# Chunked attention with two feed-forwards: an attention pair in thirteen short steps, GpSimd's lower parts in four pieces, and every second tile of the first feed-forward on ScalarE

## The chip, the cores and the metric

One core of a Trainium2 chip runs the whole program. The metric is device time in microseconds (us) of one execution, shown as the median of several runs. The engines are called as in the profile: PE is TensorE, DVE is VectorE, ACT is ScalarE, POOL is GpSimd, and SP is the engine whose queue issues most transfers. Each engine takes its own instructions strictly in order and waits for the others by semaphores.

## What is computed

Attention within chunks of 64 tokens, then two feed-forwards of 4608 tokens, width 512 and inner width 2048, in float32:

```python
def _attn_ref(q, k, v):            # q, k, v: (8, 8, 576, 64), chunks of 64
    scores = scale * np.matmul(q_c, k_c.transpose(0, 1, 2, 4, 3))
    scores = scores - np.max(scores, axis=-1, keepdims=True)
    attn = np.exp(scores)
    attn = attn / (np.sum(attn, axis=-1, keepdims=True) + 1e-09)
    out = np.matmul(attn, v_c)

def _moe_ref(x, w_in, w_out, s, b):
    r = np.maximum(x @ w_in, 0.0)
    return (s * (r * r) + b) @ w_out

def _moe2_ref(x, w_in, w_out):
    h = x @ w_in
    return (h * (1.0 / (1.0 + np.exp(-1.702 * h)))) @ w_out
```

## The kernel before, in words

The tokens are cut into nine blocks of 512. A product in full precision is made of three matmuls in a reduced type: each operand is split into an upper part (`hi`, `gh`, `xh`) and a lower part (`lo`, `gl`, `xl`), and lo x hi, hi x hi and hi x lo are summed in PSUM.

A block of a feed-forward runs over 16 slices i of the inner width. `gemm_in` makes h for one slice with twelve matmuls of 128x512 (line 519), two PSUM banks in turn. In the first feed-forward, h becomes g = s * relu(h)^2 + b and is split (lines 531 to 536): ACT makes r = relu(h), DVE r = s * r * r, ACT the upper part gh = r + b, and DVE the lower part gl = (r + b) - gh. `gemm_out` takes gh and gl, again with twelve matmuls (line 594), two slices later (`LAG`), so that on PE the slices' products alternate: twelve for h of slice i + 2, twelve for the output of slice i. There are three buffers for gh and gl.

While the first feed-forward of blocks 2 to 8 runs, three other works share the engines. The attention of the blocks still to come is done in pairs of heads (class `Pair`, a generator whose steps are placed in time by `plan_attention`, four pairs to a block): q and k are transposed in blocks of 32x32 by DVE (line 272, `qt` and `kt`), PE makes the scores (line 307), DVE subtracts the maxima and later divides by the sums (lines 316 to 329), ACT makes the exponential (line 322), DVE transposes the result with eight instructions (`turn`, line 281, `pt`), PE makes the products with v (line 292), and ACT and DVE split them (`split_x`). Second, the weights of the second feed-forward come as 64-bit numbers in two halves: SP loads them into a staging buffer `wst` (lines 112 and 118), ACT and DVE decode them into `wm` (lines 124 to 134), POOL adds (line 136) and writes them to DRAM (line 182). Third, `sums` reads four quarters of two such weights back (line 195), POOL makes sums of them (lines 198 to 201), copies the seven results to upper parts (line 203), makes the lower parts (line 204), and writes both to DRAM (line 209). `wst` has three buffers, which loads and sums take in turn. One round of this work takes two weights (the first and the second decoding) and two sums, and there are 16 rounds, 13.3 units of the plan apart (32 units are a block, two are a slice).

Then come the second feed-forward of block 0 and, from some 1050 us on, that of the other eight blocks in pairs, by products of sums of quarters (class `Halves`), which reads what `sums` wrote.

What sets the order: the plan gives every item a place in time, the code is written out in that order, and the language's scheduler then orders the instructions of each engine by its own estimate of when each could run. The steps of a pair that are due at one time are written together. `tmp` has ten buffers for all passing tiles of 128x512.

Names: `r`, `gh`, `gl` as above; `p` the scores, `sm` their sums, `pt` the transposed scores; `wst` and `wm` the staged and the decoded weight; `acc` the PSUM banks of the outputs; `ost` the output on its way to DRAM.

Of the kernel before, what the change touches and what calls it, by code (L numbers as in the profile page):

```python
# [8 lines left out]
F32 = mybir.dt.float32  # L9
F32R = mybir.dt.float32r  # L10
# [14 lines left out]


FIRST_STEPS = (0, 0.6, 0.8, 1.1, 1.8, 2.4, 2.7, 3.6, 3.9, 4.5)
LAG = 2
STAGED = 8
OPS = 4  # L30
# [16 lines left out]
def chunk_attention_two_ffn(ctx, tc, q, k, v, w1_in, w1_out, s, b, w2_in, w2_out, out):  # L47
# [50 lines left out]
    def split(hi, lo, src):  # L98

        nc.scalar.activation(out=hi, in_=src, func=AF.Copy)  # L100
        nc.vector.tensor_tensor(out=lo, in0=src, in1=hi.bitcast(F32), op=ALU.subtract)


    def tmp(name, dtype=F32):
        return tpool.tile([P, NB_MAX], dtype, tag="tmp", name=name)
# [83 lines left out]
    def sums(kind, i, z):  # L189

        q = staged().rearrange("p f z -> p (f z)").bitcast(F32).rearrange("p (t c) -> p t c", c=P)
        one, two = ((1, 2), (0, 3)) if kind == "wi" else ((1, 0), (2, 3))
        for t, (a, b) in ((i, one), (i + KF // 2, two)):
            for c, to in ((z, a), (2 + z, b)):
                nc.sync.dma_start(out=q[:, to, :], in_=w2_dram[kind][t][:, c * P:(c + 1) * P])
        yield
        a21, a11, a12, a22, s1, s2, s3, s4 = (q[:, t, :] for t in range(8))
        nc.gpsimd.tensor_tensor(out=s1, in0=a21, in1=a22, op=ALU.add)
        nc.gpsimd.tensor_tensor(out=s3, in0=a11, in1=a21, op=ALU.subtract)
        nc.gpsimd.tensor_tensor(out=s2, in0=s1, in1=a11, op=ALU.subtract)  # L200
        nc.gpsimd.tensor_tensor(out=s4, in0=a12, in1=s2, op=ALU.subtract)
        hi = staged().rearrange("p f z -> p (f z)").bitcast(F32R).rearrange("p (t c) -> p t c", c=P)[:, 0:7, :]
        nc.gpsimd.tensor_copy(out=hi, in_=q[:, 1:8, :])
        nc.gpsimd.tensor_tensor(
            out=q[:, 1:8, :].bitcast(F32R), in0=q[:, 1:8, :], in1=hi.bitcast(F32), op=ALU.subtract
        )
        to = wi_sums[i][:, :, z] if kind == "wi" else wo_sums[:, :, i, z]
        for part, src in enumerate((hi.bitcast(F32), q[:, 1:8, :])):
            nc.gpsimd.dma_start(out=to[:, :, part, :], in_=src)
# [26 lines left out]
    class Pair:  # L236
# [32 lines left out]
        def stage_qk(self):  # L269
            self.qt, self.kt = tmp("qt")[:, 0:self.n], tmp("kt")[:, 0:self.n]  # L270
            for t, src in ((self.qt, self.raw[0]), (self.kt, self.raw[1])):
                nc.vector.transpose(out=t.rearrange("p (u l) -> p u l", l=BK), in_=src)
            yield
            yield

        def turn(self, p):
            pt = tmp("pt")[:, 0:self.n].rearrange("p (c t) -> p c t", t=CH)
            for r in heads:
                for eq in range(2):
                    for ek in range(2):  # L280
                        nc.vector.transpose(  # L281
                            out=pt[r.start + ek * BK:r.start + (ek + 1) * BK, :, eq * BK:(eq + 1) * BK],
                            in_=p[r.start + eq * BK:r.start + (eq + 1) * BK, :, ek * BK:(ek + 1) * BK],
                        )
            return pt

        def room_scores(self):
            return left
# [12 lines left out]
        def steps(self):  # L301

            yield from self.stage_qk()
            yield
            ps = self.room_scores().rearrange("p e (c t) -> p e c t", t=CH)
            for e, i, c, h, r, other in quarters(self.nch):
                nc.tensor.matmul(  # L307
                    out=ps[other, e, i, :], lhsT=self.qt[r, c * CH:(c + 1) * CH], rhs=self.kt[r, c * CH:(c + 1) * CH],
                    start=True, stop=True,
                )  # L310
            yield
            mx = spool.tile([P, self.nch], F32, tag="mx", name="mx")
            sm = spool.tile([P, self.nch], F32, tag="sm", name="sm")
            p = tmp("p")[:, 0:self.n].rearrange("p (c t) -> p c t", t=CH)
            by_bank = mx.rearrange("p (e c) -> p e c", e=2)
            nc.vector.tensor_reduce(out=by_bank, in_=ps, axis=AX.X, op=ALU.max)
            nc.vector.tensor_tensor(
                out=p.rearrange("p (e c) t -> p e c t", e=2), in0=ps,
                in1=by_bank.unsqueeze(3).to_broadcast([P, 2, self.nch // 2, CH]), op=ALU.subtract,
            )  # L320
            yield
            nc.scalar.activation(out=p, in_=p, func=AF.Exp, scale=scale)
            yield
            nc.vector.tensor_reduce(out=sm, in_=p, axis=AX.X, op=ALU.add)
            nc.vector.tensor_scalar(out=sm, in0=sm, scalar1=1e-9, scalar2=None, op0=ALU.add)
            nc.vector.reciprocal(out=sm, in_=sm)
            nc.vector.tensor_tensor(  # L327
                out=p, in0=p, in1=sm.unsqueeze(2).to_broadcast([P, self.nch, CH]), op=ALU.mult
            )
            yield  # L330
            turned = self.turn(p)
            yield
            self.second(turned)
            yield
            self.split_x()
            done[0, self.j] = done.get((0, self.j), 0) + 1

    class EarlyPair(Pair):
# [21 lines left out]
        def turn(self, p):  # L360
            ps = acc_ps.tile([P, self.n], F32, tag=f"acc{2 * (self.hp % 2)}", name="pT")
            for i in range(self.n // P):
                nc.tensor.transpose(
                    ps[:, i * P:(i + 1) * P], p[:, 2 * i:2 * i + 2, :].rearrange("p c t -> p (c t)"), ident
                )
            pt = tmp("pt")[:, 0:self.n]
            nc.vector.tensor_copy(out=pt, in_=ps)
            return pt.rearrange("p (c h q) -> p c h q", h=2, q=CH)


        def room_scores(self):
# [95 lines left out]
    def steps_at(times, make, after_x=False):  # L467

        st = {}

        def step(n):
            g = st.setdefault("g", make())
            traced = nc.cur_bb.bb.instructions
            old = len(traced)
            for _ in range(n):
                next(g, None)
            for ins in traced[old:] if after_x else ():
                if ins.engine in first_x:
                    tc.add_manual_dep(ins, first_x[ins.engine].name, IN_ORDER, reason="behind the first x")
        for t, n in times:  # L480
            at(t, step, n)

    def plan_attention(j):

        base = NS * (j - 1)
        for p in range(HP):
            pr, o = Pair(j, p), base + (-6 + 8 * p if j == 2 else 7 * p - 3)
            at(o - 6.5, pr.load_qk)
            at(o + 2.5, pr.load_v)
            steps_at(((o - 2, 3), (o + 1, 1), (o + 2, 4), (o + 8, 1), (o + 8.5, 1)), pr.steps)  # L490

    def plan_y(j):
        base = NS * (NBLK + j - 1)
# [17 lines left out]
    def gemm_in(f, j, i):  # L511
        n = sizes[j]
        hi, lo = W[f, "wi", i]
        assert done[f, j] == KD
        ps = h_ps.tile([P, n], F32, tag="h", name="h")
        for kk in range(KD):
            xh, xl = X[f, j, kk]
            for a, (w_, x_) in enumerate(((lo, xh), (hi, xh), (hi, xl))):
                nc.tensor.matmul(  # L519
                    out=ps, lhsT=w_[:, kk, :], rhs=x_,  # L520
                    start=kk == 0 and a == 0, stop=kk == KD - 1 and a == 2,
                )
        if f == 0 and j < 2:
            if (j, i) == (0, 1):
                first_x[mybir.EngineType.PE] = nc.cur_bb.bb.instructions[-1]
            return keep_square(j, i, ps)
        gh = gpool.tile([P, n], F32R, tag="gh", name="gh")
        gl = gpool.tile([P, n], F32R, tag="gl", name="gl")
        r = tmp("r")[:, 0:n]
        if f == 0:  # L530
            nc.scalar.activation(out=r, in_=ps, func=AF.Relu)  # L531
            nc.vector.scalar_tensor_tensor(out=r, in0=r, scalar=s_ap, in1=r, op0=ALU.mult, op1=ALU.mult)  # L532
            nc.scalar.activation(out=gh, in_=r, func=AF.Identity, bias=b_ap)  # L533
            nc.vector.scalar_tensor_tensor(  # L534
                out=gl, in0=r, scalar=b_ap, in1=gh.bitcast(F32), op0=ALU.add, op1=ALU.subtract
            )
        else:
            nc.scalar.activation(out=r, in_=ps, func=AF.Sigmoid, scale=1.702)
            nc.vector.tensor_tensor(out=r, in0=ps, in1=r, op=ALU.mult)
            split(gh, gl, r)  # L540
        return gh, gl
# [411 lines left out]
```

## Time and profile before

| | us |
|---|---|
| median of 3 runs | 1676.16 (1675.64 to 1676.69) |
| the profiled execution's own time | 1671.44 |
| its span, first to last instruction | 1669.6 |

| engine | busy us | share of the span |
|---|---|---|
| PE | 1592.9 | 95% |
| PE's weight loads | 1293.2 | 77% |
| DVE | 1183.2 | 71% |
| ACT | 720.6 | 43% |
| POOL | 364.9 | 22% |

The shares are means over stages that differ. A busy PE also counts matmuls at the lower of its two clock levels (1.2 GHz instead of 2.4), so the granted clock is read beside it; a clock of 0.98 means that a small part of the stretch ran at half speed. In a timeline, the number in brackets is the idle time of the engine in front of the instruction, with what ended it.

### The profile page before, as it was taken

To read this page: it belongs to the slowest core of one execution; us is meant where nothing else is said; L and a number is where in the kernel's file an instruction comes from. 1 tells how busy PE (TensorE), PEld (TensorE's weight loads), DVE (VectorE), ACT (ScalarE), POOL (GpSimd) and SP (SyncE) were. 2 spreads that over 40 slices of the span, in tenths; PEclk is the share of its full clock that TensorE was granted. 3 is DMA by queue.
4 is the path that set the end of the run, shared out by engine and by line. 5 is a ranking of instruction groups with operands and counts; after the bars stand their busy time and mean duration, and the time that the engine had idled before them with its cause. 6 is when DMAs were issued, how large, how long until landed. Compare 5 with 4: busy or idle time off the path is not lost.

```text
span 1669.6 us, 24650 instructions
## 1 busy us (share of the span) xinstructions
PE 1592.9 (95%) x8928; PEld 1293.2 (77%) x8928; DVE 1183.2 (71%) x1832; ACT 720.6 (43%) x1222; POOL 364.9 (22%) x390
## 2 busy tenths in 40 slices
PE   5889999999999999899999999999999999999998
PEld 4668877787877788678888888888887888788876
DVE  5786757878766787777866644469667956894685
ACT  3668634323322333223334533446345534553552
POOL 1322101444444434344454210000000000100000
PEclk8889999999999999899999999999999999999999
DMA  9425444545455454545337551576767686768663
GB/s 231 110 101 149 129 130 124 149 136 152 124 145 137 120 151 126 149 127 151 103 118 223 167 161 35 182 227 228 201 210 251 195 224 204 243 180 239 209 202 76
DMA packets 348937, 272.19 MB, mean 163 GB/s; under 512 B 256144, under 2 KB 288912, under 8 KB 348816
## 3 DMA queue, kind: packets, MB, share of 16 engines
q1 hardware_dynamic: 333200, 220.28, 47.3%
q0 software_dynamic: 13312, 46.15, 8.3%
q10 hardware_dynamic: 2304, 4.20, 0.7%
q8 instruction: 70, 1.15, 0.3%
q14 instruction: 51, 0.42, 0.1%
HBM read 209.72 MB, written 60.82 MB: 162 GB/s over the span
## 4 chain that ended last, share of the span: by engine, by line
PE 51%; DVE 1%; ACT 0%; issue 0%; ACTq 0%
PE x L789 10%; PE x L694 10%; PE acc L594 7%; PE h L519 7%; PE at L694 5%; PE at L789 5%; PE b L694 3%; PE b L789 3%; DVE wo L716 0%; DVE pt L281 0%; ACT r L715 0%; PE at L292 0%; PE at L307 0%; DVE p L327 0%; DVE gl L534 0%
## 5 line engine op out<-in xcount | busy, mean ns | idle before, releaser
L519 PE MATMUL h<-xh,wi 128*128 128x512 f32 x1280 | 404.5, 398 | 10.0 <-ACT r L549 8.6
L594 PE MATMUL acc<-gh,wo 128*128 128x512 f32 x1152 | 363.0, 403 | 15.3 <-ACT gh L533 8.8
L519 PEld LDWEIGHTS h<-xh,wi 128*128 128x128 f32 x1280 | 242.3, 191 | 63.8 <-ACT r L549 10.1
L594 PEld LDWEIGHTS acc<-gh,wo 128*128 128x128 f32 x1152 | 220.8, 194 | 65.1 <-ACT gh L533 10.6
L519 PE MATMUL h<-xl,wi 128*128 128x512 f32 x640 | 251.9, 394 | 0.0
L594 PE MATMUL acc<-gl,wo 128*128 128x512 f32 x576 | 225.4, 402 | 12.3 <-DVE gl L534 12.2
L533 ACT ACTIVATE gh<-r,sb 128x512 fp32r<-128x512 f32 x112 | 80.9, 723 | 235.0 <-DVE r L532 234.7
L534 DVE SCALAR_TENSOR_TENSOR gl<-r,sb,gh 128x512 fp32r<-128x512 f32 x112 | 113.2, 1012 | 50.7 <-ACT gh L533 50.7
L594 PEld LDWEIGHTS acc<-gl,wo 128*128 128x128 f32 x576 | 111.3, 193 | 40.6 <-DVE gl L534 17.1
L519 PEld LDWEIGHTS h<-xl,wi 128*128 128x128 f32 x640 | 122.1, 191 | 26.2
L630 POOL DMA_DIRECT2D xr<-y x32 | 17.6, 549 | 506.7 <-ACT r L715 242.4
L532 DVE SCALAR_TENSOR_TENSOR r<-r,sb 128x512 f32<-128x512 f32 x112 | 109.0, 976 | 21.8 <-ACT r L531 21.3
L136 POOL TENSOR_TENSOR wm<-wm,wc 128x512 int32<-128x512 int32 x52 | 77.8, 1498 | 211.1 <-DVE wm L134 140.4
L716 DVE TENSOR_TENSOR wo<-wo,r 128x512 f32<-128x512 f32 x96 | 66.1, 692 | 74.4 <-ACT r L715 74.0
L766 ACT ACTIVATE op<-wo 128x512 fp32r<-128x512 f32 x128 | 80.1, 631 | 79.3 <-PE x L789 28.2
L789 PE MATMUL x<-op,wi 128*128 128x512 f32 x432 | 105.1, 389 | 0.0
L281 DVE STREAM_TRANSPOSE pt<-p 32x256 f32<-32x256 f32 x224 | 97.7, 436 | 4.1
L531 ACT ACTIVATE r<-h 128x512 f32<-128x512 f32 x112 | 65.8, 587 | 77.7 <-PE h L519 69.4
L694 PE MATMUL x<-xh,wi 128*128 128x512 f32 x320 | 99.0, 389 | 0.0
L715 ACT ACTIVATE r<-wo 128x512 f32<-128x512 f32 x96 | 60.8, 633 | 88.2 <-DVE wo L713 87.4
L767 DVE TENSOR_TENSOR op<-wo,op 128x512 fp32r<-128x512 f32 x128 | 86.0, 680 | 11.8 <-ACT op L766 10.4
L789 PEld LDWEIGHTS x<-op,wi 128*128 128x128 f32 x432 | 81.1, 188 | 16.8
(149 smaller groups left out, 2786.5 us busy)
## 6 DMA issues: line engine op xcount, KB each, us to landing
wi<-wo_sums SPq DMA_DIRECT2D x112, 512.0 KB, 3.8
wi<-wi_sums SPq DMA_DIRECT2D x96, 512.0 KB, 3.6
wst<-in_moe_w_out SPq DMA_DIRECT2D x32, 512.0 KB, 3.8
wi_sums<-wst POOLq DMA_DIRECT2D x32, 448.0 KB, 4.3
wo_sums<-wst POOLq DMA_DIRECT2D x32, 448.0 KB, 4.2
wst<-in_moe_w_in SPq DMA_DIRECT2D x24, 512.0 KB, 4.2
y<-ost SPq DMA_DIRECT2D x36, 256.0 KB, 3.2
xr<-y POOLq DMA_DIRECT2D x32, 256.0 KB, 4.4
```

The lines of the kernel that those rows point to most:

```text
L136: nc.gpsimd.tensor_tensor(out=t, in0=t, in1=c.bitcast(I32), op=ALU.add)
L281: nc.vector.transpose(out=pt[r.start + ek * BK:r.start + (ek + 1) * BK, :, eq * BK:(eq + 1) * BK], in_=p[r.start + eq * BK:r.start + (eq + ...
L519: nc.tensor.matmul(out=ps, lhsT=w_[:, kk, :], rhs=x_, start=kk == 0 and a == 0, stop=kk == KD - 1 and a == 2,)
L532: nc.vector.scalar_tensor_tensor(out=r, in0=r, scalar=s_ap, in1=r, op0=ALU.mult, op1=ALU.mult)
L533: nc.scalar.activation(out=gh, in_=r, func=AF.Identity, bias=b_ap)
L534: nc.vector.scalar_tensor_tensor(out=gl, in0=r, scalar=b_ap, in1=gh.bitcast(F32), op0=ALU.add, op1=ALU.subtract)
L594: nc.tensor.matmul(out=acc[m], lhsT=l_, rhs=r_, start=i == 0 and a == 0, stop=i == KF - 1 and a == 2)
L694: nc.tensor.matmul(out=self.ps[key], lhsT=l_, rhs=r_, start=start and k == 0 and a == 0, stop=k == HK - 1 and a == 2, skip_group_check=not ...
L716: nc.vector.tensor_tensor(out=g, in0=h, in1=r, op=ALU.mult)
L766: nc.scalar.activation(out=hi, in_=src, func=AF.Copy)
L767: nc.vector.tensor_tensor(out=lo, in0=src, in1=hi.bitcast(F32), op=ALU.subtract)
L789: nc.tensor.matmul(out=self.ps[key], lhsT=l_, rhs=r_, start=start and i == 0 and a == 0, stop=i == HF - 1 and a == 2, skip_group_check=not ...
```

## The change

Three edits, on DVE, POOL and ACT. A pair's steps are given one by one with times of their own (`PAIR_STEPS`, in plan units from the pair's place), where they were given in five groups: the two transposes of q and k at -2 and -1.5, the scores at 1, maximum and subtraction at 1.9, the exponential at 2.2, the division at 3, the eight transposes in twos at 3.7, 4.2, 4.7 and 5.2, the second product at 8 and the split at 8.5 (maximum to last transpose were all at 2). The early pairs of blocks 0 and 1 have the same number of steps as before, at the same times. POOL's lower parts of 7 x 128 columns are made with four instructions, of two, two, two and one tile of 128 columns. In the first feed-forward of blocks 2 to 8, the odd slices (56 of 112) get r = r^2 and then s * r + b on ACT, and `split`: the upper part by an ACT copy and the lower by a DVE subtraction.

```diff
@@ -25,6 +25,7 @@
 
 
 FIRST_STEPS = (0, 0.6, 0.8, 1.1, 1.8, 2.4, 2.7, 3.6, 3.9, 4.5)
+PAIR_STEPS = (-2, -1.5, -1, 1, 1.9, 2.2, 3, 3.7, 4.2, 4.7, 5.2, 8, 8.5)
 LAG = 2
 STAGED = 8
 OPS = 4
@@ -201,9 +202,12 @@
         nc.gpsimd.tensor_tensor(out=s4, in0=a12, in1=s2, op=ALU.subtract)
         hi = staged().rearrange("p f z -> p (f z)").bitcast(F32R).rearrange("p (t c) -> p t c", c=P)[:, 0:7, :]
         nc.gpsimd.tensor_copy(out=hi, in_=q[:, 1:8, :])
-        nc.gpsimd.tensor_tensor(
-            out=q[:, 1:8, :].bitcast(F32R), in0=q[:, 1:8, :], in1=hi.bitcast(F32), op=ALU.subtract
-        )
+
+        for t0, t1 in ((0, 2), (2, 4), (4, 6), (6, 7)):
+            nc.gpsimd.tensor_tensor(
+                out=q[:, 1 + t0:1 + t1, :].bitcast(F32R), in0=q[:, 1 + t0:1 + t1, :], in1=hi[:, t0:t1, :].bitcast(F32),
+                op=ALU.subtract,
+            )
         to = wi_sums[i][:, :, z] if kind == "wi" else wo_sums[:, :, i, z]
         for part, src in enumerate((hi.bitcast(F32), q[:, 1:8, :])):
             nc.gpsimd.dma_start(out=to[:, :, part, :], in_=src)
@@ -270,11 +274,11 @@
             self.qt, self.kt = tmp("qt")[:, 0:self.n], tmp("kt")[:, 0:self.n]
             for t, src in ((self.qt, self.raw[0]), (self.kt, self.raw[1])):
                 nc.vector.transpose(out=t.rearrange("p (u l) -> p u l", l=BK), in_=src)
-            yield
-            yield
+                yield
 
         def turn(self, p):
-            pt = tmp("pt")[:, 0:self.n].rearrange("p (c t) -> p c t", t=CH)
+
+            self.pt = pt = tmp("pt")[:, 0:self.n].rearrange("p (c t) -> p c t", t=CH)
             for r in heads:
                 for eq in range(2):
                     for ek in range(2):
@@ -282,7 +286,7 @@
                             out=pt[r.start + ek * BK:r.start + (ek + 1) * BK, :, eq * BK:(eq + 1) * BK],
                             in_=p[r.start + eq * BK:r.start + (eq + 1) * BK, :, ek * BK:(ek + 1) * BK],
                         )
-            return pt
+                    yield
 
         def room_scores(self):
             return left
@@ -328,9 +332,8 @@
                 out=p, in0=p, in1=sm.unsqueeze(2).to_broadcast([P, self.nch, CH]), op=ALU.mult
             )
             yield
-            turned = self.turn(p)
-            yield
-            self.second(turned)
+            yield from self.turn(p)
+            self.second(self.pt)
             yield
             self.split_x()
             done[0, self.j] = done.get((0, self.j), 0) + 1
@@ -365,7 +368,8 @@
                 )
             pt = tmp("pt")[:, 0:self.n]
             nc.vector.tensor_copy(out=pt, in_=ps)
-            return pt.rearrange("p (c h q) -> p c h q", h=2, q=CH)
+            self.pt = pt.rearrange("p (c h q) -> p c h q", h=2, q=CH)
+            yield
 
 
         def room_scores(self):
@@ -487,7 +491,8 @@
             pr, o = Pair(j, p), base + (-6 + 8 * p if j == 2 else 7 * p - 3)
             at(o - 6.5, pr.load_qk)
             at(o + 2.5, pr.load_v)
-            steps_at(((o - 2, 3), (o + 1, 1), (o + 2, 4), (o + 8, 1), (o + 8.5, 1)), pr.steps)
+
+            steps_at([(o + t, 1) for t in PAIR_STEPS], pr.steps)
 
     def plan_y(j):
         base = NS * (NBLK + j - 1)
@@ -529,6 +534,12 @@
         r = tmp("r")[:, 0:n]
         if f == 0:
             nc.scalar.activation(out=r, in_=ps, func=AF.Relu)
+            if i % 2:
+
+                nc.scalar.activation(out=r, in_=r, func=AF.Square)
+                nc.scalar.activation(out=r, in_=r, func=AF.Identity, scale=s_ap, bias=b_ap)
+                split(gh, gl, r)
+                return gh, gl
             nc.vector.scalar_tensor_tensor(out=r, in0=r, scalar=s_ap, in1=r, op0=ALU.mult, op1=ALU.mult)
             nc.scalar.activation(out=gh, in_=r, func=AF.Identity, bias=b_ap)
             nc.vector.scalar_tensor_tensor(
```

How the scheduler's order moves shows best on DVE, at three places. The first is a pair of block 7, whose eight transposes stand ahead of r of a tile whose gh PE waits for at 750.06. Before:

```order
L327 TENSOR_TENSOR p_7251<-p_7251,sm_7250 128x512
L281 STREAM_TRANSPOSE pt_7259<-p_7251 32x8x32 x8
L125 TENSOR_SCALAR wm_7309<-wst_7268 128x512
L532 SCALAR_TENSOR_TENSOR r_7292<-r_7292,sb_95 128x512
L128 SCALAR_TENSOR_TENSOR wm_7309<-wst_7268,wm_7309 128x512
L134 SCALAR_TENSOR_TENSOR wm_7309<-wst_7268,wm_7309 128x512
L534 SCALAR_TENSOR_TENSOR gl_7291<-r_7292,sb_95,gh_7290 128x512
```

Now:

```order
L331 TENSOR_TENSOR p_7354<-p_7354,sm_7353 128x512
L285 STREAM_TRANSPOSE pt_7403<-p_7354 32x8x32 x2
L543 SCALAR_TENSOR_TENSOR r_7382<-r_7382,sb_95 128x512
L285 STREAM_TRANSPOSE pt_7403<-p_7354 32x8x32 x2
L126 TENSOR_SCALAR wm_7408<-wst_7358 128x512
L285 STREAM_TRANSPOSE pt_7403<-p_7354 32x8x32 x4
L545 SCALAR_TENSOR_TENSOR gl_7381<-r_7382,sb_95,gh_7380 128x512
L129 SCALAR_TENSOR_TENSOR wm_7408<-wst_7358,wm_7408 128x512
L135 SCALAR_TENSOR_TENSOR wm_7408<-wst_7358,wm_7408 128x512
```

The tile (now `r_7382`) has its r behind two transposes and its gl behind all eight; the first decoding step of a weight (`wm_7408`) stands between them. At the pair whose transposes stood ahead of the r that PE waits for at 549.15, r now stands ahead of all eight, and gl behind them.

The second place is the pair in front of the wait at 704.95. Before:

```order
L327 TENSOR_TENSOR p_6827<-p_6827,sm_6826 128x512
L281 STREAM_TRANSPOSE pt_6835<-p_6827 32x8x32 x8
L532 SCALAR_TENSOR_TENSOR r_6866<-r_6866,sb_95 128x512
L534 SCALAR_TENSOR_TENSOR gl_6865<-r_6866,sb_95,gh_6864 128x512
L272 STREAM_TRANSPOSE qt_6905<-qs_6717 128x512
L272 STREAM_TRANSPOSE kt_6906<-ks_6718 128x512
L125 TENSOR_SCALAR wm_6909<-wst_6871 128x512
```

Now:

```order
L331 TENSOR_TENSOR p_6920<-p_6920,sm_6919 128x512
L285 STREAM_TRANSPOSE pt_6970<-p_6920 32x8x32 x8
L102 TENSOR_TENSOR gl_6945<-r_6946,gh_6944 128x512
L276 STREAM_TRANSPOSE qt_6997<-qs_6807 128x512
L126 TENSOR_SCALAR wm_7000<-wst_6956 128x512
L276 STREAM_TRANSPOSE kt_6998<-ks_6808 128x512
L543 SCALAR_TENSOR_TENSOR r_6990<-r_6990,sb_95 128x512
```

The tile behind the eight transposes is an odd one now: no r is made on DVE, and the subtraction for gl follows the transposes. The next even tile's r stands behind one decoding step and both transposes of the next pair's q and k.

The third place is a decoding in front of the wait at 481.01. Before:

```order
L125 TENSOR_SCALAR wm_4704<-wst_4657 128x512
L532 SCALAR_TENSOR_TENSOR r_4674<-r_4674,sb_95 128x512
L128 SCALAR_TENSOR_TENSOR wm_4704<-wst_4657,wm_4704 128x512
L134 SCALAR_TENSOR_TENSOR wm_4704<-wst_4657,wm_4704 128x512
L534 SCALAR_TENSOR_TENSOR gl_4673<-r_4674,sb_95,gh_4672 128x512
```

Now:

```order
L543 SCALAR_TENSOR_TENSOR r_4708<-r_4708,sb_95 128x512
L126 TENSOR_SCALAR wm_4750<-wst_4691 128x512
L129 SCALAR_TENSOR_TENSOR wm_4750<-wst_4691,wm_4750 128x512
L545 SCALAR_TENSOR_TENSOR gl_4707<-r_4708,sb_95,gh_4706 128x512
L135 SCALAR_TENSOR_TENSOR wm_4750<-wst_4691,wm_4750 128x512
```

r is ahead of the decoding's first step now, and gl ahead of its last. On PE the order from 300 us on is the same in both; on POOL the four pieces stand together where the one instruction stood.

## Rows read from the trace of the kernel before

**Rows 1.** The page, section 1: busy us (share of the span) x instructions.

```profile
PE 1592.9 (95%) x8928; PEld 1293.2 (77%) x8928; DVE 1183.2 (71%) x1832; ACT 720.6 (43%) x1222; POOL 364.9 (22%) x390
```

**Rows 2.** Two stretches: us; busy us of PE, PEld, DVE, ACT, POOL; clock, DMA, GB/s.

```profile
300.00:760.00 460.00, 435.38 (x2893) 349.87 (x2888) 347.43 (x526) 141.67 (x232) 205.42 (x219) 0.96 0.52 138
760.00:1050.00 290.00, 289.95 (x1510) 238.59 (x1509) 184.61 (x258) 110.73 (x184) 90.16 (x100) 1.00 0.45 139
```

**Rows 3.** Waits of PE, 300 to 760 us: us in total, times, longest.

```profile
PE acc L594 <- DVE gl L534: 12.2, 7, 2.6
PE acc L594 <- ACT gh L533: 8.8, 3, 4.6
```

**Rows 4.** Timeline of PE: start, us, line, tiles, count [idle before <- releaser].

```profile
399.34 0.51 PE L594 MATMUL acc<-gl,wo 128*128 128x512 f32 x1 [2.55 <-DVE gl L534]
...
481.01 0.49 PE L594 MATMUL acc<-gl,wo 128*128 128x512 f32 x1 [1.91 <-DVE gl L534]
...
528.78 0.50 PE L594 MATMUL acc<-gl,wo 128*128 128x512 f32 x1 [2.25 <-DVE gl L534]
...
549.15 0.73 PE L594 MATMUL acc<-gh,wo 128*128 128x512 f32 x2 [2.59 <-ACT gh L533]
...
693.67 0.80 PE L594 MATMUL acc<-gl,wo 128*128 128x512 f32 x1 [2.33 <-DVE gl L534]
...
704.95 1.22 PE L594 MATMUL acc<-gh,wo 128*128 128x512 f32 x2 [4.61 <-ACT gh L533]
...
750.06 0.73 PE L594 MATMUL acc<-gh,wo 128*128 128x512 f32 x2 [1.62 <-ACT gh L533]
```

**Rows 5.** Timeline of DVE, a decoding and the gl behind it.

```profile
687.98 0.43 DVE L125 TENSOR_SCALAR wm<-wst 128x512 int32<-128x512 int32 x1 [7.64 <-DMA wst<-in_moe_w_in]
...
689.71 1.42 DVE L134 SCALAR_TENSOR_TENSOR wm<-wst,wm 128x512 f32<-128x512 f32 x1
691.05 2.56 DVE L534 SCALAR_TENSOR_TENSOR gl<-r,sb,gh 128x512 fp32r<-128x512 f32 x1
```

**Rows 6.** Timeline of POOL: four of the lower parts; 300.06 and 761.55 begin rounds.

```profile
300.06 2.58 POOL L204 TENSOR_TENSOR wst<-wst 128x896 fp32r<-128x896 f32 x1
...
677.08 2.12 POOL L204 TENSOR_TENSOR wst<-wst 128x896 fp32r<-128x896 f32 x1
...
690.66 2.40 POOL L204 TENSOR_TENSOR wst<-wst 128x896 fp32r<-128x896 f32 x1
...
761.55 2.12 POOL L204 TENSOR_TENSOR wst<-wst 128x896 fp32r<-128x896 f32 x1
```

**Rows 7.** Timeline of DVE, the transposes ahead of the wait at 704.95.

```profile
699.77 3.58 DVE L281 STREAM_TRANSPOSE pt<-p 32x256 f32<-32x256 f32 x8
703.39 0.75 DVE L532 SCALAR_TENSOR_TENSOR r<-r,sb 128x512 f32<-128x512 f32 x1
704.93 0.75 DVE L534 SCALAR_TENSOR_TENSOR gl<-r,sb,gh 128x512 fp32r<-128x512 f32 x1 [0.79 <-ACT gh L533]
```

**Rows 8.** Waits of SP's queue, 300 to 760 us.

```profile
SPq L112 <- DMA wo_sums<-wst: 30.2, 7, 7.3
```

**Rows 9.** Groups by line and form, whole span: busy us, mean ns | idle before.

```profile
L532 DVE SCALAR_TENSOR_TENSOR r<-r,sb 128x512 f32<-128x512 f32 x112 | 109.0, 976 | 21.8 <-ACT r L531 21.3
L534 DVE SCALAR_TENSOR_TENSOR gl<-r,sb,gh 128x512 fp32r<-128x512 f32 x112 | 113.2, 1012 | 50.7 <-ACT gh L533 50.7
L101 DVE TENSOR_TENSOR gl<-r,gh 128x512 fp32r<-128x512 f32 x16 | 11.1, 692 | 8.6 <-ACT gh L100 8.4
L533 ACT ACTIVATE gh<-r,sb 128x512 fp32r<-128x512 f32 x112 | 80.9, 723 | 235.0 <-DVE r L532 234.7
L557 ACT ACTIVATE r<-r 128x512 f32<-128x512 f32 x16 | 10.0, 624 | 0.1
L570 ACT ACTIVATE wo<-wo,sb 128x512 f32<-128x512 f32 x16 | 12.8, 804 | 0.0
L100 ACT ACTIVATE gh<-r 128x512 fp32r<-128x512 f32 x16 | 10.1, 633 | 11.1 <-DVE r L539 11.0
```

**Rows 10.** Instructions on wst, POOL, 300 to 760 us: duration ns min/median/max.

```profile
L200 POOL TENSOR_TENSOR wst<-wst x22: 458/621/982, 303.4 to 758.3; 128x128 f32<-128x128 f32 x22
```

## The prediction

> **What bounds the kernel now.** I read the page's busy times first: TensorE (PE) is busy for 95% of the span [rows 1], so time is to be had only where PE waits or runs at the lower of its two clock levels. The table by stretches comes next. From 760 us on PE has no idle time and a granted clock of 1.00. From 300 to 760 us, where the first feed-forward of blocks 2 to 8 runs with the attention of later blocks and the second feed-forward's weights, PE is busy 435.38 of 460 us at a mean clock of 0.96 [rows 2]. That is 24.6 us idle, and 0.04 x 460 = 18.4 us lost at 1.2 GHz, which follows the waits: 0.75 us for each us of idle time. So some 43 us can be won here, and nothing later.
>
> The waits of PE in that stretch name two things, gl by VectorE (DVE) and gh by ScalarE (ACT) [rows 3]. PE's timeline shows seven large ones in two kinds [rows 4]. Four (2.55, 1.91, 2.25, 2.33; 9.0 us) wait for gl. At the last of them DVE has stood 7.64 us for the load of wst, and then its gl takes 2.56 us where the same instruction takes 0.75 us elsewhere [rows 5, 7]; it ends when GpSimd's (POOL's) lower part does, 690.66 + 2.40 [rows 6]. The three others (2.59, 4.61, 1.62; 8.8 us) wait for gh, and gh waits for r on DVE: at 704.95 r stands behind the eight transposes of one pair, 3.58 us [rows 7]. Idle time outside these seven is 24.6 - 17.9 = 6.7 us.
>
> Behind both lies a ring. A weight's load needs a staging buffer that POOL's sums must first write out; SP waits for that [rows 8], decoding needs the load, and the next sums need the decoded weight. From the lower part at 300.06 to that at 761.55 there are eleven turns [rows 6], 41.95 us each; without 43 us of loss PE would need 38.0 per turn.
>
> **The change, part by part.** Durations are from the groups by line [rows 9] unless another group is named. The sum is made against the profiled execution, 1671.44 us (span 1669.6), which is 4.7 under the median of the three runs, 1676.16.
>
> *Odd tiles on ScalarE.* 56 of 112 tiles lose two DVE instructions (0.976 + 1.012) and get a subtraction (0.692): 1.30 us less each, 73 us in all, about 47 of DVE's 347 in the stretch [rows 2]. ACT loses 0.723 and gets Square 0.624, Identity with two pointers 0.804 and the copy 0.633: 1.34 more, 48 us on 142, so it stays under half busy. The chain h to gl keeps its length (DVE 1.99 + ACT 0.72 against ACT 2.06 + DVE 0.69), but it crosses from ACT to DVE once, not three times, and stands in DVE's queue once. In itself I cost this at nothing; the cover is the two tiles of matmuls between h and its use. If ACT is held, by the same wst load at the head of its queue, four instructions of an odd tile stand behind it.
>
> *Short lower parts.* 128 columns take 0.46 (the least of the adds [rows 10]) and 896 take 2.12 [rows 6], so 256 take about 0.46 + 1.66/6 = 0.74. A DVE instruction that meets them waits for one piece, not for the rest of 2.40. The four gl come earlier by between 1.07 (a whole piece) and 1.81 each: 4.3 to 7.2. The order moves too: at 693.67 the gl stays behind wm's two steps, elsewhere a wm step goes behind gl. I take 6.0 us; with 0.75 of clock for each, **-10.5** (ends -4, no clock back, and 9.0 x 1.75 = -15.8).
>
> The price: four pieces take 3 x 0.74 + 0.46 = 2.68, 0.56 more per sum. At three seams DVE may come in, and POOL waits. The adds of 128 columns, four single instructions in a row, range from 0.458 to 0.982 [rows 10], so up to 0.52 a seam, 1.6 a sum. "SBUF — State Buffer" of the Trainium skill, section "Who interferes with whom", says that whoever starts first holds the shared ports for the whole instruction; by that a seam costs up to a whole DVE instruction, 0.75 here, and a sum 2.3. The largest stretch seen, 0.52, is under it. The sum is made without that page. Bounds: 0 where the ring doesn't set the pace, 22 x (0.56 + 1.6) = 47 where it does in both sums of each turn. The first sum of a turn comes while DVE stands waiting (2.12 at 677.08 [rows 6]), so I take near the lower end, two thirds of 11 x 0.56: **+4**.
>
> *The pair's steps.* Eight transposes may now be parted. The order shows how far: at the stall of 549.15 r now stands ahead of all eight, at 750.06 behind two, and at 704.95 the tile is odd and needs no r from DVE, while the eight stay together; in several pairs the next pair's qt and kt come in between. Each gl is earlier by r's 0.75 and the 0.79 until gh is there, 1.5 to 1.8 us [rows 7], 4.9 for the three; with the clock **-8.6** (ends 0, where the late load of 687.98 moves everything behind it, and 8.8 x 1.75 = -15.4).
>
> *The rest.* Of the other 6.7 us a part goes because DVE catches up sooner: **-4** (ends 0 and -11.8). PE's own order in the stretch is as before. On SP some loads of q and k change places with staged loads by a few rows, and the early pairs' turn only changes its form; both at nothing, covered by loads that SP holds back anyway [rows 8]. If that cover goes, a staged load is later by a group of four issues, and the ring with it.
>
> Sum: -10.5 + 4 - 8.6 - 4 = -19.1, so 1652.3 for the profiled execution and, with its 4.7, **1657** for the median.
>
> **The rivals.** *The eight still block* (the change doesn't do what it says, since six to eight transposes stand together in most pairs): the -8.6 fails, 1666. For it: the order. Against: no odd tile waits for r there.
>
> *All waits go*: 1676.2 - 43 = 1633. For it: every wait of the stretch ends with DVE. Against: the load that DVE waits for 7.64 us is not made earlier.
>
> *The ring sets the pace*: if a turn stays near 42 us, a PE that waits less here waits more at the next wst, and only the earlier gl counts, about 4: 1672. For it: 11 turns x 3.95 are just the 43 us lost. Against: of DVE's part in a turn (decoding behind tiles) some is taken away.
>
> *Slower, by the seams*: POOL's first sum in each turn, where what leaves the buffer decides the next load, grows by 0.56 + 1.6 = 2.1; over eleven turns +23, less -10.5 for the gl: 1689. It decides from the point where a turn gets longer than today's 41.95 us. For it: SP waits for just these writes [rows 8]. Against: in the first sum DVE mostly stands.
>
> *Slower, by ScalarE*: Square and Identity take 1.43 where DVE took 0.976; if all 56 odd gh were on the path, 0.45 x 56 = +25, 1701. Against: ACT idles 234.7 us before gh, waiting for DVE's r [rows 9]. "ScalarE: Activation LUTs" of the Trainium skill, "Rules for kernel authors", says to put multiplications and additions on VectorE and not on ScalarE; the trace bears it out for one instruction (0.804 against 0.692), not for a queue that is held up by another engine.
>
> **How the numbers follow.** Forecast 0.50, still blocked 0.12, all gone 0.08, ring 0.15, seams 0.12, ScalarE 0.03. A measurement of this kernel can tell about 0.2%, 3.4 us. Faster: the first three and half of the ring's case, 0.77; same: the other half and a little of the seams, 0.08; slower: 0.15. The range from 1634 to 1678 leaves out both slower cases and a little at the fast end; the forecast's own is 1645 to 1668.
>
> **What would show it.** Right: gl beside the pieces under 1.5 us; the idle time of 300 to 760 under 14 us and its clock at 0.98; DVE under 310 us and ACT near 190 there; the waits for gh of odd tiles rare; a turn of the ring near 40 us. Wrong: lower parts of 3.5 us or more in four pieces and a turn over 42 (seams); fewer stalls at gl but new ones behind wst (ring); PE waiting for gh with ACT busy in front of it (ScalarE); r or gl again ending a wait behind six transposes (blocked). Any change after 1000 us beyond a shift would also go against this account.

## The result and the profile after

The changed kernel took 1690.13 us, the median of four runs (1689.02 to 1692.32), against 1675.9 for the kernel before on the same chip: 1.0094 times, 95% interval 1.0069 to 1.0118, so **0.9% slower**. The prediction had said 1657, faster.

The page of the changed kernel: busy times and instructions (section 1), then, from section 4, the chain that ended last by engine and by line.

```profile
PE 1597.1 (94%) x8928; PEld 1293.6 (77%) x8928; DVE 1100.7 (65%) x1776; ACT 791.5 (47%) x1334; POOL 386.9 (23%) x486
...
PE 58%; DMA 11%; POOL 9%; DVE 8%; issue 7%; SPq 6%; ACT 3%; POOLq 0%; DVEq 0%; ACTq 0%
```

Against [rows 1], VectorE lost 82 us and ScalarE gained 71, as the change says; POOL gained 22. PE still leads the chain, but POOL and the transfers have a fifth of it. The table by stretches says where (columns as in [rows 2]):

```profile
300.00:760.00 460.00, 430.25 (x2831) 345.69 (x2830) 290.39 (x488) 185.54 (x301) 212.28 (x276) 0.96 0.52 136
760.00:960.00 200.00, 189.27 (x1030) 151.35 (x1029) 115.61 (x172) 91.67 (x152) 98.25 (x126) 0.97 0.49 150
960.00:1060.00 100.00, 100.00 (x443) 82.81 (x442) 42.90 (x65) 39.72 (x65) 5.31 (x9) 1.00 0.33 100
```

The same stretch of the kernel before:

```profile
760.00:960.00 200.00, 199.95 (x1113) 164.04 (x1112) 146.13 (x201) 81.12 (x135) 85.74 (x92) 1.00 0.50 155
```

PE is busy 5.1 us less than before in the first stretch, at the same clock, and 10.7 us less in the second, where the granted clock fell from 1.00 to 0.97 (0.03 x 200 = 6 us). Together 21.8 us; the span grew by 20.9 (1669.6 to 1690.5). From 960 us on nothing but a shift is left. So three quarters of the loss lie in a stretch where the prediction saw nothing to win, and so looked for nothing to lose.

PE's waits from 300 to 760 us (us, times, longest), against [rows 3]:

```profile
PE acc L605 <- ACT gh L544: 9.0, 1, 9.0
PE acc L605 <- DVE gl L102: 5.9, 4, 2.8
PE h L524 <- ACT r L536: 5.8, 2, 3.0
PE acc L605 <- ACT gh L101: 5.0, 3, 2.7
PE acc L605 <- DVE gl L545: 2.5, 2, 1.9
```

The waits for gl fell from 12.2 to 8.4 us, and one single wait of 9 us for gh, at 703 us, came in their place. It is a late weight of the second feed-forward that shows through DVE. DVE, ACT and SP ahead of it, from their timelines (start, us, ... [idle before <- releaser]):

```profile
699.33 0.88 DVE L126 TENSOR_SCALAR wm<-wst 128x512 int32<-128x512 int32 x1 [18.58 <-DMA y<-ost]
700.25 1.09 DVE L129 SCALAR_TENSOR_TENSOR wm<-wst,wm 128x512 int32<-128x512 int32 x1
701.26 0.94 DVE L543 SCALAR_TENSOR_TENSOR r<-r,sb 128x512 f32<-128x512 f32 x1
...
696.11 0.66 ACT L125 ACTIVATE wc<-wst 128x512 int32<-128x512 uint32 x1 [13.69 <-DMA wst<-in_moe_w_in]
...
691.77 0.39 SPq L113 DMA_DIRECT2D wst<-in_moe_w_in  x1
692.20 1.03 SPq L256 DMA_DIRECT2D qs<-in_q  x2
693.33 2.43 SPq L256 DMA_DIRECT2D ks<-in_k  x3
695.86 0.42 SPq L617 DMA_DIRECT2D y<-ost  x1
```

SP could issue the load of wst only at 691.77. ACT stood 13.7 us for it. Behind it in SP's queue stood the outputs (`y<-ost`); they and wm share the ten passing buffers, and the row names the leaving of an output as what ended DVE's 18.6 us. r and gh stood behind both. SP had waited 8.4 us for the write of a sum, POOL's work:

```profile
SPq L113 <- DMA wo_sums<-wst: 8.4, 1, 8.4
```

The chain of waits shows the whole loop. From 760 to 960 us, before, it is nearly PE alone (it reaches back to 795 us):

```profile
by line: PE acc L594 38.2%; PE h L519 37.7%; DVE pt L281 1.3%; PE at L292 0.9%; issue 0.6%; PE at L307 0.5%; DVE p L327 0.4%; DVE r L532 0.4%; DVE gl L534 0.4%; ACT gh L533 0.4%; DVE p L317 0.4%; DVE sm L324 0.3%; ACT p L322 0.3%; DVE mx L3
```

and in the changed kernel it is the ring, piece by piece (start, us, what):

```profile
782.49 3.43 POOL wst L207 x4
785.92 0.84 POOL wo_sums L213
786.76 2.97 issue
789.74 0.90 POOL wo_sums L213
790.65 1.33 POOL wm L137
791.98 2.07 issue
794.05 3.22 DMA w_wi<-wm
```

Sum, transfer, POOL's wait before the next transfer, decoding, the decoded weight's write, and then the next sum's load: that goes on to the last round. I measure a turn as the time from the copy that precedes a lower part, in the first sum of a round, to the same in the next. First and last of the sixteen rounds, before:

```profile
296.12 0.93 POOL L203 CAST wst<-wst 128x896 fp32r<-128x896 f32 x1
...
915.98 0.94 POOL L203 CAST wst<-wst 128x896 fp32r<-128x896 f32 x1
```

and after:

```profile
294.19 0.93 POOL L204 CAST wst<-wst 128x896 fp32r<-128x896 f32 x1
...
936.31 0.93 POOL L204 CAST wst<-wst 128x896 fp32r<-128x896 f32 x1
```

Fifteen turns of 41.32 us before and of 42.81 after: 22.3 us more. The first round began 1.9 us earlier, and what follows the last takes nearly the same time in both, 753.6 and 754.2 us: together the 20.9 of the span.

The lower parts themselves, whole in [rows 6] and now in pieces: groups by form from 290 to 960 us (busy us, mean ns | idle before). Before:

```profile
L204 POOL TENSOR_TENSOR wst<-wst 128x896 fp32r<-128x896 f32 x32 | 74.3, 2322 | 1.4
```

After:

```profile
L207 POOL TENSOR_TENSOR wst<-wst 128x256 fp32r<-128x256 f32 x96 | 85.8, 920 | 1.4
L207 POOL TENSOR_TENSOR wst<-wst 128x128 fp32r<-128x128 f32 x32 | 20.9, 653 | 0.0
```

(85.8 + 20.9) / 32 = 3.33 us per sum against 2.32: 1.0 us more, and two sums per turn.

### The profile page after: what moved, and what is told of

It is laid out like the page before. It is cut to its first block, busy times and chain, and to the rows that moved or that the text cites. A ratio compares the mean times of both kernels' runs of the same rounds, so it can differ in the third digit from the quotient of the medians.

```text
span 1690.5 us, 24775 instructions
## 1 busy us (share of the span) xinstructions
PE 1597.1 (94%) x8928; PEld 1293.6 (77%) x8928; DVE 1100.7 (65%) x1776; ACT 791.5 (47%) x1334; POOL 386.9 (23%) x486
## 4 chain that ended last, share of the span: by engine, by line
PE 58%; DMA 11%; POOL 9%; DVE 8%; issue 7%; SPq 6%; ACT 3%; POOLq 0%; DVEq 0%; ACTq 0%
PE acc L605 11%; PE x L800 10%; PE x L705 10%; PE h L524 10%; PE at L705 5%; PE at L800 5%; POOL wst L207 4%; PE b L800 3%; PE b L705 3%; SPq L256 3%; DMA wi_sums<-wst 2%; DMA wo_sums<-wst 2%; DMA wst<-w_wo 1%; SPq L269 1%; DVE pt L285 1%
## 5 line engine op out<-in xcount | busy, mean ns | idle before, releaser
L137 POOL TENSOR_TENSOR wm<-wm,wc 128x512 int32<-128x512 int32 x52 | 73.6, 1416 | 196.7 <-DVE wm L135 170.9
L126 DVE TENSOR_SCALAR wm<-wst 128x512 int32<-128x512 int32 x52 | 25.3, 492 | 124.1 <-DMA wst<-in_moe_w_in 59.4
L207 POOL TENSOR_TENSOR wst<-wst 128x256 fp32r<-128x256 f32 (+1 forms) x128 | 105.5, 853 | 1.4
L544 ACT ACTIVATE gh<-r,sb 128x512 fp32r<-128x512 f32 x56 | 40.5, 723 | 114.2 <-DVE r L543 114.1
```

The lines of the kernel that those rows point to most:

```text
L137: nc.gpsimd.tensor_tensor(out=t, in0=t, in1=c.bitcast(I32), op=ALU.add)
L207: nc.gpsimd.tensor_tensor(out=q[:, 1 + t0:1 + t1, :].bitcast(F32R), in0=q[:, 1 + t0:1 + t1, :], in1=hi[:, t0:t1, :].bitcast(F32), op=ALU.s ...
```

## The experiments

Theory **S** (seams): DVE comes in between the pieces, lower parts get longer, and with them the ring's turn. Theory **O** (order): it is the new order, on DVE and ACT and SP, that makes stalls such as the one at 703 us. Later, theory **R** (the ring of staging buffers sets the pace) against **V** (VectorE's queue does).

**The change without the pieces.**

```
-        for t0, t1 in ((0, 2), (2, 4), (4, 6), (6, 7)):
-            nc.gpsimd.tensor_tensor(out=q[:, 1 + t0:1 + t1, :]..., op=ALU.subtract)
+        nc.gpsimd.tensor_tensor(out=q[:, 1:8, :]..., in0=q[:, 1:8, :], in1=hi..., op=ALU.subtract)
```

> The change without its short pieces: one lower part of 896 columns again. Theory S (seams): the pieces alone make a sum on GpSimd about 1 us longer (3.30 instead of 2.32 us in all), the ring of staging, decoding and sums turns slower by it, and the other two edits help; expected 1655 to 1668 us, a ring turn of 41 us or less. Theory O (order): the new order on VectorE and SP (a decoding's first step ahead of transposes, loads of q and k ahead of staged loads) delays the ring, and the pieces matter little; expected 1685 to 1692 us.

Measured: 1666.67 us, 0.9931 times before (0.991 to 0.9952), turn 41.11. The rest of the change is a gain of 0.7%; the pieces turn it into a loss of 0.9%. The edit hardly moves the order (6 of 1776 DVE instructions and 22 of 1257 transfers of SP change place against the whole change).

**The pieces alone**, in the kernel before (the same lines, the other way):

> The kernel before with the four pieces alone; the order of all engines stays nearly as before. S: 1685 to 1700 us, the lower parts of a sum 3.2 us or more in total, the ring turn about 43 us, some waits for gl shorter. O: 1662 to 1676 us, since gl gets in between the pieces and nothing else moves.

Measured: 1697.5 us, 1.0117 (1.0096 to 1.0137), turn 43.20, lower parts 3.5 us on average. Alone, too, they lose, with DVE's order nearly that of before (9 of 1832 instructions change place).

**The odd tiles on ScalarE alone** (only the block `if i % 2:` is added):

> The kernel before with the odd tiles on ScalarE alone. S: VectorE is relieved and nothing is added to the ring, 1655 to 1668 us. O: part of the new order comes with this edit, 1676 to 1690 us.

Measured: 1678.84 us, 1.0006 (0.9988 to 1.0024), turn 41.61. A miss for S: no gain.

**The pair's steps alone** (only `PAIR_STEPS` and the moved `yield`s):

> The kernel before with the pair's steps one by one alone. S: 1666 to 1676 us, a small gain or none. O: 1680 to 1692 us, with VectorE waiting for wst in front of transposes.

Measured: 1679.55 us, 1.0004 (0.999 to 1.0019), turn 41.88. No loss, which speaks against O, and no gain either, where S had allowed a small one. Each is worth nothing alone and both together 0.7%; why the turn falls only with both (41.61, 41.88, and 41.11) stays open.

**The ring relieved, in the kernel before.** POOL waits, in the trace of before, ahead of the second transfer of nearly every sum and ahead of many transfers of decoded weights, with nothing that the profile names (waits of POOL, 300 to 960 us; us, times, longest):

```profile
POOL wi_sums L209 <- issue: 48.7, 16, 5.0
POOL wo_sums L209 <- issue: 37.8, 15, 3.3
...
POOL w_wi L182 <- issue: 20.8, 6, 4.6
POOL w_wo L182 <- issue: 19.4, 7, 3.6
```

So the upper part's transfer is issued ahead of the lower part's subtraction, and the two transfers no longer stand together:

```
         nc.gpsimd.tensor_copy(out=hi, in_=q[:, 1:8, :])
+        to = wi_sums[i][:, :, z] if kind == "wi" else wo_sums[:, :, i, z]
+        nc.gpsimd.dma_start(out=to[:, :, 0, :], in_=hi.bitcast(F32))
         nc.gpsimd.tensor_tensor(out=q[:, 1:8, :].bitcast(F32R), ..., op=ALU.subtract)
-        for part, src in enumerate((hi.bitcast(F32), q[:, 1:8, :])):
-            nc.gpsimd.dma_start(out=to[:, :, part, :], in_=src)
+        nc.gpsimd.dma_start(out=to[:, :, 1, :], in_=q[:, 1:8, :])
```

> The kernel before, with the transfer of the upper parts issued ahead of the lower parts instead of behind them; nothing is left out or added. Theory R (the ring of staging, decoding and sums sets the time up to its last round, some 754 us ahead of the end): a staging buffer comes free about 2.3 us earlier in each sum, the turn falls from 41.3 to about 38.5 us, the last round starts some 40 us earlier, 1640 to 1655 us. Theory V (VectorE's queue alone sets the waits of PE): no change, 1670 to 1680 us.

Measured: 1656.18 us, 0.9866 (0.9846 to 0.9885), turn 40.16: just short of R's 1640 to 1655 and far from V's. Such waits of POOL around `wst` in its trace (tile wst, the same stretch; us, times):

```profile
  issue: 21.9, 12
```

Of the 40.2 us ahead of the decoded weights' transfers, 27.3 stayed. DVE's work was left as it was (26 of its 1832 instructions change place; the mean of gl even rose from 1012 to 1167 ns), and 1.3% came off. So the ring held up the kernel before as well, not merely the changed one.

**The same edit in the change without the pieces:**

> The change without its pieces, with the early transfer of the upper parts. R: VectorE's relief and the shorter ring add up, 1632 to 1648 us, near the bound where PE waits for nothing (1633). V: as without the early transfer, 1662 to 1670 us.

Measured: 1642.15 us, 0.9784 (0.9744 to 0.9825), turn 39.52.

**The same edit in the whole change:**

> The whole change, pieces too, with the early transfer of the upper parts. R: the pieces still cost, but behind a transfer that runs already; the turn falls from 42.8 to about 39.5 us, 1640 to 1660 us. V: 1685 to 1692 us.

Measured: 1645.31 us, 0.9803 (0.9783 to 0.9823), turn 39.82. The pieces now cost 0.3 us a turn, and their effect on the time (0.9803 against 0.9784) lies within the intervals. The four pieces still take 3.0 us here, against 2.26 for a whole lower part with this edit, but the turn grows by 0.3 us and not by 1.7 as without it (42.81 against 41.11). What the pieces cost depends on where the ring waits, not on their length alone.

**Two pieces**, in the kernel before: the loop over `((0, 4), (4, 7))`.

> The kernel before with two pieces (four and three tiles of 128 columns) instead of four: one seam instead of three. Seams theory: a third of the cost of the four pieces alone, turn 41.9 us, +5 to +9 us on the kernel before, about 1683 us. If the cost is not by seams but from the moment that VectorE gets in at all, nearly the whole of the four pieces' +19 us, about 1695 us.

Measured: 1684.46 us, 1.0033 (1.0013 to 1.0052), turn 42.32. Its lower parts:

```profile
L206 POOL TENSOR_TENSOR wst<-wst 128x512 fp32r<-128x512 f32 x32 | 48.2, 1505 | 1.3
L206 POOL TENSOR_TENSOR wst<-wst 128x384 fp32r<-128x384 f32 x32 | 43.2, 1350 | 0.0
```

2.86 us per sum, 0.53 more than whole; twice that is the 1.0 us by which the turn grew. One seam costs about half of what three cost in the ring (1.0 against 1.9 us a turn), and 0.33% against 1.17% in time, near the third that the seams theory gave.

**More space for POOL's transfers, in the whole change:**

```
-    nc = bacc.Bacc("TRN2", ..., dynamic_dma_scratch_size=1024)
+    nc = bacc.Bacc("TRN2", ..., dynamic_dma_scratch_size=2048)
```

> The whole change as it is, with twice the room for GpSimd's transfer descriptors (2048 instead of 1024); nothing else. In the change GpSimd stands some 2.8 us before the second transfer of a sum (83.5 us in 29 waits that end with nothing in the profile). Theory R: if those waits come from that room they go, the second upper part starts and the next loads come sooner, the turn falls from 42.8 to about 40 us, 1645 to 1665 us. If they are not a matter of that room, or the ring is not the bound: 1685 to 1692 us.

Measured: 1641.11 us, 0.9793 (0.9771 to 0.9816), turn 39.09: better than R had given. No such wait stands ahead of a transfer any more; what is left around `wst` stands ahead of the sums' arithmetic:

```profile
POOL wst L200 <- issue: 8.1, 3, 3.9
```

**Both edits, without the pieces:**

> The change without its pieces, with the early transfer of the upper parts and twice the room for descriptors. R: the turn falls below what PE needs (38), PE waits for little, 1630 to 1640 us. If that room does not matter: 1640 to 1645 us, as without it.

Measured: 1632.09 us, 0.9748 (0.9729 to 0.9766), turn 38.58, not under 38.

**The space alone, in the kernel before:**

> The kernel before with 2048 instead of 1024 for the space of the GpSimd queue's transfers, nothing else. R (the ring of staging buffers is the bound, and GpSimd's wait before a sum's second transfer lies in it): that wait, 90.6 us over 32 sums in the kernel before, goes, the turn falls from 41.3 to 38.5-40 us, and the time is 1635-1655, at or under that of the early transfer alone (1656). If the wait before the second transfer only hides a wait behind it: 1670 or more, turn over 41.

Measured: 1646.68 us, 0.9814 (0.9788 to 0.9841), turn 39.45, as R said. Every engine runs its instructions in the order of before, so no reordering can be the reason. Its first stretch, against [rows 2]:

```profile
300.00:760.00 460.00, 447.65 (x3012) 361.83 (x3011) 347.60 (x552) 150.00 (x244) 210.55 (x230) 0.99 0.57 146
```

PE stands idle 12.4 us there instead of 24.6, with DVE as busy as before. In this setting the whole change gains nothing that can be told (0.9793); without its pieces it gains 1.0% (0.9715, next).

**The space, in the change without the pieces:**

> The change with whole lower parts and 2048 for the space of the transfers (beside the whole change with 2048, 1641). If the pieces' price is a fixed lengthening of a turn, it is as much here as without the space (1.6% between the change and the change without pieces): 1613-1620, turn near 37.7-38. If it is paid only as far as the ring is the bound, then PE's own work is the bound here and little is left of it: 1630-1640, turn 38.4-39, PE's idle time in 300-860 under 8 us.

Measured: 1630.89 us, 0.9715 (0.9686 to 0.9745), turn 38.60 in the profiled execution, which was the longest of five (1638.26). This and the one with both edits are the **best versions**, 2.5 to 2.9% under the kernel before. Its stretches:

```profile
300.00:760.00 460.00, 454.33 (x3141) 368.80 (x3141) 322.56 (x523) 203.48 (x330) 211.44 (x233) 1.00 0.58 150
760.00:960.00 200.00, 200.00 (x1028) 164.92 (x1027) 122.15 (x174) 101.29 (x166) 74.32 (x86) 1.00 0.51 158
```

PE waits 5.7 us in all, under the 8 expected, and runs at a clock of 1.00: now PE is the bound. The pieces still cost something here, 0.9793 against 0.9715, 0.5 us a turn; part of their price is hidden, not all.

A fourth buffer for staging, the plainest test of the ring, was not run.

## Why the prediction was wrong

**What bounds the kernel: partly right, and wrong where it mattered.** The idle time lies where I said and shows as waits for gl and gh. But the late load behind one of the seven stalls was the ring's doing, and so was about half of all the idle time: with more space for POOL's transfers alone, 24.6 us became 12.4. DVE and ACT stand for wst, and in-order queues hand that on to gl and gh. With POOL's transfers alone relieved, the kernel before took 1.3% to 1.9% less.

**"And nothing later".** This sentence allowed a cost only from 300 to 760 us, eleven turns. From 760 us on PE had no idle time in the kernel before, so there was nothing to win; the ring came round there in 38.9 us without holding PE up (four turns, 761.55 to 917.00). The change made its turns 42.3 (769.94 to 939.27, lower parts, four turns), and PE had to wait. A gain ends at the idle time; a loss ends only at the slack, which the prediction never counted.

**Odd tiles on ScalarE: right locally.** DVE's busy time in the stretch fell to 290.39 (347 - 47 was expected to be 300) and ACT's rose to 185.54. Alone the edit gave nothing, as costed. PE waited three times for an odd gh, 5.0 us, and twice for ACT's r, 5.8 us, far from the 25 of the rival "ScalarE".

**Short lower parts, the gain: right locally for gl, without effect.** A gl meets a shorter block, though the prediction's reading that gl "ends when GpSimd's (POOL's) lower part does" was 0.55 us off: it ends at 693.61 and the lower part at 693.06 [rows 5, 6]. The groups of the changed kernel by line, against [rows 9], and the same two of the change without the pieces:

```profile
L543 DVE SCALAR_TENSOR_TENSOR r<-r,sb 128x512 f32<-128x512 f32 x56 | 46.2, 825 | 23.3 <-ACT r L536 23.0
L545 DVE SCALAR_TENSOR_TENSOR gl<-r,sb,gh 128x512 fp32r<-128x512 f32 x56 | 47.9, 856 | 25.8 <-ACT gh L544 25.6
...
L540 DVE SCALAR_TENSOR_TENSOR r<-r,sb 128x512 f32<-128x512 f32 x56 | 46.5, 830 | 20.3 <-ACT r L533 19.9
L542 DVE SCALAR_TENSOR_TENSOR gl<-r,sb,gh 128x512 fp32r<-128x512 f32 x56 | 54.4, 971 | 25.8 <-ACT gh L541 25.6
```

The mean of r fell from 976 to 825 ns and that of gl from 1012 to 856. For r the pieces have no part in it (830 without them); for gl they have most (971 without them). Of the -10.5 no run shows anything in the time: the pieces cost net in the ring as it was, and gain nothing even where the ring is relieved (0.9803 against 0.9784, 0.9793 against 0.9715).

**Short lower parts, the price: the step that failed.** The prediction wrote: "The first sum of a turn comes while DVE stands waiting (2.12 at 677.08 [rows 6]), so I take near the lower end, two thirds of 11 x 0.56: **+4**." The size of a seam was right: four undisturbed pieces take 2.55 us (2.68 was expected), and with three seams up to 4.36 (2.68 + 1.6 = 4.28 was the upper bound). What was wrong is how often DVE comes in, and in which sums. Of 32 sums only seven take the undisturbed time; the first sums of a turn take 3.0 us on average and the second 3.6, and the second is in the chain like the first. One row showed a waiting DVE; I took it for the rule, though the same group has a first sum of 2.58 (300.06). For gain and price together the prediction had -6.5 us (-10.5 + 4); measured: +27 us with the rest of the change (1.0094 against 0.9931), +1.17% alone.

How DVE comes in is best seen at 910 us. POOL, then DVE, in the changed kernel:

```profile
910.32 4.36 POOL L207 TENSOR_TENSOR wst<-wst 128x256 fp32r<-128x256 f32 x4
...
910.89 1.20 DVE L153 TENSOR_TENSOR wi<-wm,wi 128x512 fp32r<-128x512 f32 x1
912.01 1.21 DVE L102 TENSOR_TENSOR gl<-r,gh 128x512 fp32r<-128x512 f32 x1
913.14 1.22 DVE L543 SCALAR_TENSOR_TENSOR r<-r,sb 128x512 f32<-128x512 f32 x1
```

Three DVE instructions that take 0.69 to 0.75 us undisturbed take 1.2 each, one to a seam, and the four pieces take 1.8 us more: the two engines go by turns. A whole lower part never took over 2.58 in the kernel before: it has no seams. "SBUF — State Buffer" of the Trainium skill, section "Who interferes with whom", says that whoever issues first has the shared ports for the whole instruction. The trace agrees: 0.6 us for a seam, about one DVE instruction of 0.7. The prediction had set that page's price (2.3 a sum) aside as the larger one; at two sums a turn even its own 0.52 a seam was enough for the loss.

**The pair's steps and the rest: right in sum, wrong apart.** -8.6 - 4 = -12.6 was forecast, and without the pieces the change gives 0.9931, -11.6 us. But the steps alone give nothing, and the odd tiles alone nothing; the forecast had the -8.6 come from the steps by themselves. Its working also priced gl (1.5 to 1.8 us earlier) where the three waits named gh. That the sums agree is luck.

**The rivals.** What happened is "slower, by the seams", 1689 forecast and 1690 measured, its condition met: over the same eleven turns 42.97 us (297.30 to 769.94), against 41.95. Its chance of 0.12 was too low, for the reason given. Its working was not wholly right either: it counted eleven turns and one sum of each, and set the gl against it; fifteen turns and both sums count, at 0.75 us net per sum. So the closeness of 1689 is partly luck. "The ring sets the pace" was right too, as the mechanism behind it; I had held it for a case of its own and given the sum the chances of a kernel without a ring. "ScalarE" and "eight still block" did not decide.

**What would show it.** Of the signs, gl beside the pieces under 1.5 us, DVE under 310, ACT near 190 and few waits for an odd gh came; the turn, the idle time (29.8, not under 14) and the clock (0.96, not 0.98) did not. The ring's sign came too: fewer waits at gl and a new one behind wst. The sign of the seams was 3.5 us or more in four pieces; the mean is 3.33, eight of 32 reach 3.5, and the turn is over 42.

## What to carry to other kernels

Ask of every edit on an engine with little work (POOL, 22%) whether its work stands in a loop of buffers that comes round: follow one turn through all its queues, to its last round, and compare it with what the bound engine needs per turn, also where that engine does not wait yet. Cutting an instruction into pieces helps whoever waits for the shared resource and makes the one that is cut longer; do it only where the cut one has slack. When two local gains each measure as nothing, look for a third thing that sets the pace, and relieve that first.

## What the runs showed of the hardware

*The second transfer in a row on POOL waits.* With 1024 for the space of its transfers, POOL waited 2.8 us ahead of nearly every sum's second transfer (86.5 us, 31 times) and 3.1 us ahead of many decoded weights' transfers (40.2 us, 13 times), with nothing in the profile that it waited for. With 2048 no transfer has such a wait, and the time falls by 1.9% in the kernel before and by 3.0% in the change (0.9793 against 1.0094). "DMA: Bandwidth & Descriptors" of the Trainium skill, section "SWDGE vs HWDGE vs iDMA", says that GpSimd writes a transfer's descriptors to rings in a reserved part of SBUF. That a second transfer waits for room there fits these numbers, but no run shows the rings themselves. The small space cost more (31 us) than the whole change was meant to bring (19); its sign stood in the trace before, as "issue" in front of POOL's transfers, and the prediction did not use it.
